# Full-softmax decode attention with gradients: V scores, O and dq by wide matmuls in four column groups

## The chip, the cores and the metric

The kernel runs on one core of a Trainium2 chip. The metric is device time in microseconds (us) of one execution. The median of three executions of the kernel before is 645.86 us (645.73 to 649.34).

## The reference: what is computed

One query per head, 32 heads, 8192 keys of 128 bf16 numbers. Forward attention, and its gradients for a given `grad_out` (called dO here):

```python
B, H, Sq, Skv, Dh = 1, 32, 1, 8192, 128
scores = jnp.einsum('bhqd,bhkd->bhqk', q, k) * scale      # scale = 128 ** -0.5
attn = _softmax(scores, axis=-1)
out  = jnp.einsum('bhqk,bhkd->bhqd', attn, v)
_out, _vjp = jax.vjp(_f, q, k, v)
_grads = _vjp(grad_out)                                   # dq, dk, dv
```

Written out for one head, with p the softmax row: O = p V; the "V scores" dp = V dO, one number a key; ds = p (dp - sum(p dp)) scale; dq = ds K. The two large outputs are outer products: dv = p times dO, and dk = ds times q. Each head therefore reads 2 MB of K and 2 MB of V, and writes 2 MB of dk and 2 MB of dv. All four are touched once.

## The kernel before

**Layout.** A head's K (or V) lies in SBUF as [128 partitions, 64 slots, 128 numbers]: partition p holds the 64 keys 64p to 64p+63. K has three such buffers (`K_BUFS`), V two (`V_BUFS`), and the outputs dk and dv two each (`gpool`). All loads and stores are issued by SyncE (SP) and stand in one queue in program order: a store waits there for its outer products, a load for its buffer. `load_v` (L76) fetches a head's V in one transfer, `load_k` (L71) its K.

**Order.** From L91 on the order is the one written out by hand (`manual_schedule`): each engine takes its instructions in the order of the program text. The loop over h at L260 is a software pipeline: pass h does the K side of head h, the dk and dq work of head h-1 (called `p_`), then the V side of head h.

**K side of head h.** Four VectorE 32x32-block transposes (L146, `k_blocks`) lay K out for contraction over its 128 numbers. 64 TensorE matmuls with four moving columns (L157, `k_scores`) give the scores; a mask (L163) and four matmuls into 32 partitions each (L173, `s_swap`) put them back on the partitions of their keys. Maximum (L284 to L295, with a TensorE transpose at L288), exponential and row sum (L299), the sum over partitions (L300), its reciprocal (L307); then p, four times repeated (`p_rep`, L309), and p times scale (`p_s`, L311).

**V side of head h.** V is read as f32 words, so that one 128x128 transpose on TensorE moves two bf16 slots. Four batches of eight transposes (L188, `v_transposes`) go through two PSUM tiles of two banks each; ScalarE copies each batch of 1024 words to SBUF (L179, `v_copy`), three buffers deep. The V scores are 64 matmuls with the transposed V as stationary operand and two moving columns (L200, `v_scores`), so dp lands on the partitions of its keys. O is 64 matmuls with V as it was loaded as stationary operand and one moving column of p (L205, `contract`), and a copy into a column of `o_all` (L316). The sum of p dp is had as O times dO, by one matmul (L320), before the last scores are in. Four VectorE outer products of 2048 numbers a partition make dv (L215, `outer`), and `load_v(h + 2)` is called between the third and the fourth.

**Head h-1.** ds, four times repeated, in one VectorE instruction (L241, `ds_of`); four outer products make dk; 64 matmuls make dq (L205 again, `dq_of`, in two halves around L173), copied to a column of `dq_all` (L249).

At the end, `result` (L251) turns `o_all` and `dq_all` round and stores them. Heads 0 and 31 store dk and dv in two halves.

The lines below are those that the change touches, and their callers.

Of the kernel before, what the change touches and what calls it, by code (L numbers as in the profile page):

```python
# [9 lines left out]
ALU = mybir.AluOpType  # L10
AX = mybir.AxisListType
BF16 = mybir.dt.bfloat16
F32 = mybir.dt.float32
PSUM = bass.MemoryType.PSUM

CH = 16
R = 4
K_BUFS = 3
V_BUFS = 2
QD = 32  # L20
# [3 lines left out]
def kernel(  # L24
# [11 lines left out]
    nc = tc.nc  # L36
    P = 128
    _, H, S, D = k.shape
    assert D == P and S % (P * CH) == 0 and H <= P
    NT = S // P  # L40
    NCH = NT // CH
    NQ = P // QD
    assert NCH == 4 and NQ == 4
    W = D // 2
# [3 lines left out]
    consts = ctx.enter_context(tc.tile_pool(name="consts", bufs=1))  # L48
# [3 lines left out]
    tpool = ctx.enter_context(tc.tile_pool(name="tsb", bufs=3))  # L52
    gpool = ctx.enter_context(tc.tile_pool(name="gen", bufs=2))
    small = ctx.enter_context(tc.tile_pool(name="small", bufs=2))
    psT = ctx.enter_context(tc.tile_pool(name="psT", bufs=2, space=PSUM))
    psS = ctx.enter_context(tc.tile_pool(name="psS", bufs=1, space=PSUM))
    psD = ctx.enter_context(tc.tile_pool(name="psD", bufs=2, space=PSUM))
    psM = ctx.enter_context(tc.tile_pool(name="psM", bufs=1, space=PSUM))

    Kt, Vt, XK, XV, st = {}, {}, {}, {}, {}  # L60
# [35 lines left out]
    do_blk = consts.tile([P, H, 2, 2], BF16)  # L96
    nc.vector.memset(do_blk[:], 0.0)
# [11 lines left out]
    tp = psT.tile([P, CH, P], BF16, tag="T", name="tp_q")  # L109
# [13 lines left out]
    do_f = consts.tile([P, H], F32)  # L123

    def do_columns():
        for e2 in range(2):
            nc.scalar.copy(
                twice[:, e2], rows[:, 1, :].rearrange("h (j e) -> h e j", e=2)[:, e2:e2 + 1, :].to_broadcast([H, 2, W]))
        tp = psT.tile([P, CH, P], BF16, tag="T", name="tp_do")
        for e2 in range(2):  # L130
            nc.tensor.transpose(tp[:, e2, 0:H], twice[:, e2].rearrange("h t j -> h (t j)"), ident[0:H, 0:H])
        nc.tensor.transpose(tp[:, 2, 0:H], rows[:, 1, :], ident[0:H, 0:H])
        for e2 in range(2):
            for t in range(2):
                nc.scalar.copy(do_blk[t * W:(t + 1) * W, :, e2, t], tp[t * W:(t + 1) * W, e2, 0:H])
        nc.scalar.copy(do_f[:], tp[:, 2, 0:H])
# [40 lines left out]
    def v_copy(h, c):  # L177
        X = tpool.tile([P, CH // 2, P], F32, tag="XT", name="XT_sb")
        nc.scalar.copy(X[:], st[h].pop("T")[:])  # L179
        XV[h, c] = X  # L180

    def v_transposes(h, c, copy=True):

        T_ps = psT.tile([P, CH // 2, P], F32, tag="T", name="T_ps")
        words = Vt[h].rearrange("p n d -> p (n d)").bitcast(F32)
        for i in range(CH // 2):
            m = c * CH // 2 + i
            nc.tensor.transpose(T_ps[:, i, :], words[:, m * P:(m + 1) * P], ident_f[:])  # L188
        st[h]["T"] = T_ps
        if copy:  # L190
            v_copy(h, c)

    def v_scores(h, c):
        X = XV.pop((h, c)).rearrange("p m s -> p (m s)").bitcast(BF16).rearrange("p (m s e) -> p m e s", s=P, e=2)
        if c == 0:
            st[h]["dp"] = psD.tile([P, 512], F32, tag="dp", name="dp_ps")
        for i in range(CH // 2):
            n = c * CH + 2 * i
            for e2 in range(2):
                nc.tensor.matmul(st[h]["dp"][:, n:n + 2], lhsT=X[:, i, e2, :], rhs=do_blk[:, h, e2, :],  # L200
                                 start=(e2 == 0), stop=(e2 == 1), skip_group_check=True)

    def contract(Xt, rep, out_col, first=0, last=NT):
        for n in range(first, last):
            nc.tensor.matmul(out_col, lhsT=Xt[:, n, :], rhs=rep[:, n, 0:1],  # L205
                             start=(n == 0), stop=(n == NT - 1), skip_group_check=True)
# [28 lines left out]

    def ds_of(h):
        x = st[h]
        pdt = small.tile([P, 1], F32, tag="pdt")
        nc.vector.tensor_copy(pdt[:], x["m"][:, 1:2])  # L239
        x["ds"] = small.tile([P, NT, R], BF16, tag="dsrep", name="ds_rep")  # L240
        nc.vector.scalar_tensor_tensor(  # L241
            out=x["ds"][:], in0=x["dp"][:, 0:NT].unsqueeze(2).to_broadcast([P, NT, R]), scalar=pdt[:],
            in1=x["p_s"][:].unsqueeze(2).to_broadcast([P, NT, R]), op0=ALU.subtract, op1=ALU.mult)

    def dq_of(h, half):
        out = st[h]["dp"][:, 128:129]
        contract(Kt[h], st[h]["ds"], out, half * NT // 2, (half + 1) * NT // 2)
        if half == 1:
            nc.scalar.copy(dq_all[:, h:h + 1], out)  # L249

    def result(src, dst):  # L251
        half = small.tile([P, H], BF16, tag="half", name="half")
        nc.scalar.copy(half[:], src[:])
        fin_ps = psT.tile([P, CH, P], BF16, tag="T", name="fin_ps")
        nc.tensor.transpose(fin_ps[0:H, 0, :], half[:], ident[:])
        fin_sb = small.tile([H, D], BF16, tag="fin", name="fin_sb")
        nc.scalar.copy(fin_sb[:], fin_ps[0:H, 0, :])
        nc.sync.dma_start(dst.rearrange("b h s d -> (b h s) d"), fin_sb[:])

    for h in range(H + 1):  # L260
        p_ = h - 1
        if h < H:
            x = st[h] = {}
            rows_bc(h)
            for u in range(NCH):
                k_blocks(h, u)
            k_scores(h)
# [9 lines left out]
        if h > 0:  # L277
            dq_of(p_, 1)
            outer(p_, "dk", 1)
        if 0 < h and h + 2 < H:  # L280
            load_k(h + 2)
# [11 lines left out]
        if h < H:  # L293
            nbias = small.tile([P, 1], F32, tag="nbias")
            nc.vector.tensor_reduce(nbias[:], x["m"][:, 128:256], axis=AX.X, op=ALU.max, negate=True)  # L295
            v_transposes(h, 0, copy=False)
            e = small.tile([P, NT], F32, tag="e")
            rs = small.tile([P, 1], F32, tag="rs")
            nc.scalar.activation(e[:], x["sn"], ACT.Exp, bias=nbias[:], scale=scale, accum_out=rs[:])  # L299
            nc.tensor.matmul(x["m"][:, 0:1], lhsT=ones_f[:], rhs=rs[:], start=True, stop=True,  # L300
                             skip_group_check=True)
        if h > 0:
            outer(p_, "dk", 3)
        if h == H:
            break
        rinv = small.tile([P, 1], F32, tag="rinv")
        nc.vector.reciprocal(rinv[:], x["m"][:, 0:1])  # L307
        x["p"] = small.tile([P, NT, R], BF16, tag="prep", name="p_rep")
        nc.scalar.activation(x["p"][:], e[:].unsqueeze(2).to_broadcast([P, NT, R]), ACT.Copy, scale=rinv[:])  # L309
        x["p_s"] = small.tile([P, NT], F32, tag="p_s", name="p_s")  # L310
        nc.vector.tensor_scalar(x["p_s"][:], e[:], rinv[:], scale, op0=ALU.mult, op1=ALU.mult)  # L311
        v_copy(h, 0)
        v_transposes(h, 1)
        v_transposes(h, 2)
        contract(Vt[h], x["p"], x["m"][:, 2:3])
        nc.scalar.copy(o_all[:, h:h + 1], x["m"][:, 2:3])  # L316
        v_scores(h, 0)
        v_scores(h, 1)
        v_transposes(h, 3)
        nc.tensor.matmul(x["m"][:, 1:2], lhsT=do_f[:, h:h + 1].to_broadcast([P, P]), rhs=o_all[:, h:h + 1],  # L320
                         start=True, stop=True, skip_group_check=True)
        v_scores(h, 2)
        v_scores(h, 3)
# [43 lines left out]
```

## Time and profile before

| what | value |
|---|---|
| median of three executions | 645.86 us (645.73 to 649.34) |
| span of the profiled execution, first to last instruction | 644.6 us |
| recorded instructions | 20,935, of them 9,673 matmuls and 9,673 weight loads |
| TensorE matmul busy | 482.0 us, 75% |
| VectorE busy | 505.9 us, 78% |
| ScalarE busy | 180.7 us, 28% |
| mean granted TensorE clock | 0.601 of full speed |
| moved by DMA | 269.80 MB, mean 419 GB/s |
| from issue to landing, a load of V / of K | 30.1 / 30.3 us |
| from issue to landing, a store of dv / of dk | 34.5 / 33.7 us |

How to read it: the profile is of one execution. No separate end-to-end time is recorded for that execution, so its span is set beside the median of the timed ones: 645.86 - 644.61 = 1.25 us lie around the span. Busy time of TensorE is the union of overlapping matmuls, since they are pipelined. A line such as L205 names the statement in the kernel's text; where two callers share it (O and dq do), the tile names tell them apart. In a table of windows each row is one stretch of the span, with each engine's busy time and number of instructions, the granted clock, and the mean busy share and rate of the sixteen DMA engines. In a timeline a row is: start, length, engine, line, operation, output<-inputs, shapes, count, and in brackets the idle time before it and what ended it.

### The profile page before, as it was taken

How to read it: one execution, taken by the hardware profiler on the slowest of the kernel's cores; microseconds unless marked ns; L12 is line 12 of the kernel's file. 1: busy time of each engine (PE TensorE's matmuls, PEld its weight loads, DVE VectorE, ACT ScalarE, POOL GpSimd, SP SyncE). 2: the span in 40 equal slices, each digit the busy share in tenths (PEclk: the TensorE clock that was granted, in tenths of full speed). 3: DMA queues.
4: the chain of work that ended last, by engine and by line, in shares of the span. 5: the costliest groups of instructions: out<-in, count | busy, mean ns of one | idle time of the engine just before them, and what ended most of it. 6: DMA issues, size and time to landing. Idle time of an engine off the chain costs nothing.

```text
span 644.6 us, 20935 instructions
## 1 busy us (share of the span) xinstructions
PE 482.0 (75%) x9673; PEld 443.9 (69%) x9673; DVE 505.9 (78%) x653; ACT 180.7 (28%) x332; POOL 0.7 (0%) x6
## 2 busy tenths in 40 slices
PE   3998898886777877768776787677876777877780
PEld 2887788785676766768666687567776676866670
DVE  5999899767977679867788777787767986778761
ACT  2333333322233231333222332123322233231230
POOL 0000000000000000000000000000000000000000
PEclk9666666665566655666556665566665566655665
DMA  8999999999999999999999999999999999999985
GB/s 350 404 428 429 424 427 424 428 429 421 418 429 428 428 425 430 430 426 431 425 428 428 430 426 428 428 428 427 427 429 431 424 432 424 430 426 429 427 362 244
DMA packets 19718, 269.80 MB, mean 419 GB/s; under 512 B 2352, under 2 KB 2352, under 8 KB 2864
## 3 DMA queue, kind: packets, MB, share of 16 engines
q1 hardware_dynamic: 19584, 268.47, 98.2%
q8 instruction: 75, 1.23, 0.7%
q14 instruction: 11, 0.09, 0.0%
q10 hardware_dynamic: 48, 0.01, 0.0%
HBM read 134.23 MB, written 134.23 MB: 416 GB/s over the span
## 4 chain that ended last, share of the span: by engine, by line
DMA 62%; PE 24%; DVE 9%; ACT 1%; issue 1%; SPq 0%; DVEq 0%; ACTq 0%
DMA Vt<-in_v_dram 61%; PE T_ps L188 15%; DVE XK_sb L146 4%; DVE G_dv L215 4%; PE m_ps L205 3%; PE dp_ps L200 2%; PE s_ps L157 2%; PE dp_ps L205 1%; DVE G_dk L215 1%; DMA Kt<-in_k_dram 1%; PE m_ps L300 1%; ACT p_rep L309 0%; PE s_ps L173 0%; ACT XT_sb L179 0%; PE m_ps L288 0%
## 5 line engine op out<-in xcount | busy, mean ns | idle before, releaser
L188 PE MATMUL T_ps<-ident_f,Vt 128*128 128x128 f32 x1024 | 217.0, 383 | 27.3 <-DMA Vt<-in_v_dram 24.7
L188 PEld LDWEIGHTS T_ps<-ident_f,Vt 128*128 128x128 f32 x1024 | 182.2, 206 | 45.2 <-PE m_ps L288 21.7
L215 DVE TENSOR_TENSOR G_dv<-p_rep,qd 128x2048 bf16<-128x2048 bf16 x128 | 148.2, 1220 | 60.9 <-DMA out_dram<-G_dv 52.8
L215 DVE TENSOR_TENSOR G_dk<-ds_rep,qd 128x2048 bf16<-128x2048 bf16 x128 | 155.6, 1218 | 4.6 <-DMA out_dram<-G_dk 3.6
L146 DVE STREAM_TRANSPOSE XK_sb<-Kt 128x1024 f32<-128x1024 f32 x128 | 148.3, 1214 | 5.8 <-DMA Kt<-in_k_dram 3.2
L179 ACT COPY XT_sb<-T_ps 128x1024 f32<-128x1024 f32 x128 | 128.7, 1008 | 83.9 <-PE T_ps L188 77.2
L157 PE MATMUL s_ps<-q_blk,XK_sb 128*128 128x4 bf16 x2048 | 59.8, 168 | 94.6 <-DVE pdt L239 87.6
L157 PEld LDWEIGHTS <-XK_sb 128*128 128x128 bf16 x2048 | 57.1, 104 | 103.9 <-DVE pdt L239 96.6
L200 PE MATMUL dp_ps<-do_blk,XT_sb 128*128 128x2 bf16 x2048 | 67.0, 164 | 18.0 <-ACT XT_sb L179 17.6
L200 PEld LDWEIGHTS <-XT_sb 128*128 128x128 bf16 x2048 | 65.5, 103 | 20.7 <-ACT XT_sb L179 20.2
L205 PE MATMUL dp_ps<-ds_rep,Kt 128*128 128x1 bf16 x2048 | 64.0, 165 | 0.4 <-DVE ds_rep L241 0.4
L205 PEld LDWEIGHTS <-Kt 128*128 128x128 bf16 x2048 | 59.5, 104 | 5.7 <-issue 5.6
L249 ACT COPY dq_all<-dp_ps 128x1 f32<-128x1 f32 x32 | 5.1, 159 | 205.2 <-PE dp_ps L205 182.8
L205 PEld LDWEIGHTS <-Vt 128*128 128x128 bf16 x2048 | 57.0, 96 | 0.7
L205 PE MATMUL m_ps<-p_rep,Vt 128*128 128x1 bf16 x2048 | 56.5, 163 | 0.0
L309 ACT ACTIVATE p_rep<-e,rinv 128x256 bf16<-128x256 f32 x32 | 16.3, 508 | 64.6 <-DVE rinv L307 64.6
L307 DVE RECIPROCAL rinv<-m_ps 128x1 f32<-128x1 f32 x32 | 5.4, 168 | 35.2 <-PE m_ps L300 35.1
L234 ACT CAST qd<-s_ps 128x256 bf16<-128x256 f32 x32 | 11.9, 372 | 32.5 <-PE s_ps L230 32.5
L299 ACT ACTIVATE e<-s_ps,nbias 128x64 f32<-128x64 f32 x32 | 10.1, 314 | 32.5 <-DVE nbias L295 32.5
L241 DVE SCALAR_TENSOR_TENSOR ds_rep<-dp_ps,pdt,p_s 128x256 bf16<-128x256 f32 x32 | 15.5, 484 | 4.6 <-PE dp_ps L200 1.3
L163 DVE TENSOR_TENSOR sm<-s_ps,in_quad 128x256 f32<-128x256 f32 x32 | 13.6, 425 | 6.0 <-PE s_ps L157 2.0
L300 PEld LDWEIGHTS m_ps<-rs,ones_f 128*128 128x128 f32 x64 | 17.6, 334 | 0.0
(44 smaller groups left out, 153.1 us busy)
## 6 DMA issues: line engine op xcount, KB each, us to landing
Vt<-in_v_dram SPq DMA_DIRECT2D x32, 2048.0 KB, 30.1
Kt<-in_k_dram SPq DMA_DIRECT2D x31, 2048.0 KB, 30.3
out_dram<-G_dv SPq DMA_DIRECT2D x30, 2048.0 KB, 34.5
out_dram<-G_dk SPq DMA_DIRECT2D x30, 2048.0 KB, 33.7
out_dram<-G_dv SPq DMA_DIRECT2D x4, 1024.0 KB, 14.4
out_dram<-G_dk SPq DMA_DIRECT2D x4, 1024.0 KB, 13.2
Kt<-in_k_dram SPq DMA_DIRECT2D x4, 512.0 KB, 5.1
out_dram<-fin_sb SPq DMA_DIRECT2D x2, 8.0 KB, 12.8
```

Source lines behind the costliest of these rows:

```text
L146: nc.vector.transpose(XK[h][:, :, :, u, :], slots(Kt[h], u, NCH).rearrange("p g d -> p (g d)").bitcast(F32).rearrange("p (g w j) -> p g w ...
L157: nc.tensor.matmul(out[:, g, :], lhsT=cols[:, g, c // 2, c % 2], rhs=q_blk[:, h, c, :], start=(c == 0), stop=(c == 2 * NB - 1), skip_group ...
L163: nc.vector.tensor_tensor(x["sm"][:], x["s"][:, 0:NT].rearrange("p (a g) -> p a g", a=NQ).unsqueeze(2) .to_broadcast([P, NQ, NCH, CH]), in ...
L179: nc.scalar.copy(X[:], st[h].pop("T")[:])
L188: nc.tensor.transpose(T_ps[:, i, :], words[:, m * P:(m + 1) * P], ident_f[:])
L200: nc.tensor.matmul(st[h]["dp"][:, n:n + 2], lhsT=X[:, i, e2, :], rhs=do_blk[:, h, e2, :], start=(e2 == 0), stop=(e2 == 1), skip_group_chec ...
L205: nc.tensor.matmul(out_col, lhsT=Xt[:, n, :], rhs=rep[:, n, 0:1], start=(n == 0), stop=(n == NT - 1), skip_group_check=True)
L215: nc.vector.tensor_tensor(slots(G, r, 4).rearrange("p n (a b) -> p n a b", b=R), slots(rep, r, 4).unsqueeze(2).to_broadcast([P, Q, D // R, ...
L234: nc.scalar.copy(x["qd"][:].rearrange("p a d -> p (a d)"), x["s"][:, 256:512])
L241: nc.vector.scalar_tensor_tensor(out=x["ds"][:], in0=x["dp"][:, 0:NT].unsqueeze(2).to_broadcast([P, NT, R]), scalar=pdt[:], in1=x["p_s"][: ...
L300: nc.tensor.matmul(x["m"][:, 0:1], lhsT=ones_f[:], rhs=rs[:], start=True, stop=True, skip_group_check=True)
L309: nc.scalar.activation(x["p"][:], e[:].unsqueeze(2).to_broadcast([P, NT, R]), ACT.Copy, scale=rinv[:])
```

## The change

Three groups of 64 narrow matmuls become three groups of 16 matmuls with 512 moving columns. In each the stationary operand has 32 columns, and the output is one of four groups of 32 PSUM partitions (b = 0 to 3).

- **V scores.** dO sits in a 34-column window of zeros (`do_win`), so that a slice of 32 columns puts the two scores of a slot pair in row 0 and 1, or 2 and 3, of the group. The moving operand is transposed V, every second bf16, 16 x 32 numbers. The result has the keys along the free dimension; a VectorE 32x32-block transpose of [128, 512] f32 from PSUM (`v_back`) puts it back on the partitions.
- **O and dq.** p (or ds) sits in the last four columns of a window of zeros (`wins`, two for each); the slice is chosen so that head h writes rows 4 (h mod 8) to 4 (h mod 8) + 3 of its group. The moving operand is V (or K) as loaded, four slots at a time. Eight heads add up in one PSUM bank; after every eighth head a copy and four small matmuls (`gather`) add the 16 partial rows of each head.
- **The sum of p dp** is taken from dp itself: a product with e on VectorE, accumulated along the row (L218 of the changed kernel), one matmul with ones (`pd_sum`), times 1/sum. It no longer uses O.
- **ds** is made once (64 numbers a partition) and then copied four times over; ScalarE copies it into its window. p is copied into its window too.
- **Transposes of V** are eight batches of four (one bank each, three in rotation) in place of four batches of eight; all of transposed V of a head is kept, in one SBUF buffer.
- The windows are cleared by GpSimd at the start; the memset of `do_win` stands ahead of the second step of the identity matrix in GpSimd's order.

```diff
+TB = 4
+ST = 8
-    psT = ctx.enter_context(tc.tile_pool(name="psT", bufs=2, space=PSUM))
+    xvpool = ctx.enter_context(tc.tile_pool(name="xvp", bufs=1))
+    single = ctx.enter_context(tc.tile_pool(name="single", bufs=1))
+    psT = ctx.enter_context(tc.tile_pool(name="psT", bufs=3, space=PSUM))
-    psD = ctx.enter_context(tc.tile_pool(name="psD", bufs=2, space=PSUM))
+    psD = ctx.enter_context(tc.tile_pool(name="psD", bufs=1, space=PSUM))
+    psO = ctx.enter_context(tc.tile_pool(name="psO", bufs=1, space=PSUM))
+    psQ = ctx.enter_context(tc.tile_pool(name="psQ", bufs=1, space=PSUM))
...
+    do_win = consts.tile([P, H, 2, QD + 2], BF16)
+    nc.gpsimd.memset(do_win[:], 0.0)
+            w = consts.tile([P, NG, 2 * QD - 4], BF16, name=f"win_{which}{i}")
+            nc.gpsimd.memset(w[:], 0.0)
...
-    def v_scores(h, c):
-        X = XV.pop((h, c)).rearrange(...)
-        for i in range(CH // 2):
-            n = c * CH + 2 * i
-            for e2 in range(2):
-                nc.tensor.matmul(st[h]["dp"][:, n:n + 2], lhsT=X[:, i, e2, :], rhs=do_blk[:, h, e2, :],
-                                 start=(e2 == 0), stop=(e2 == 1), skip_group_check=True)
+    def v_scores(h):
+        cols = XV.pop(h).rearrange(...)("p (m z s e) -> p z e m s", z=2, s=P, e=2)
+        for z in range(2):
+            for e2 in range(2):
+                for b in range(NQ):
+                    nc.tensor.matmul(out[b * QD:(b + 1) * QD, :], lhsT=do_win[:, h, e2, 2 - 2 * z:2 - 2 * z + QD],
+                                     rhs=cols[:, z, e2, :, b * QD:(b + 1) * QD], ...)
...
+    def v_back(h):
+        nc.vector.transpose(x["dpT"][:].rearrange("p m r -> p (m r)"), x["dp"][:])
+        nc.vector.scalar_tensor_tensor(
+            out=prod[:], in0=x["dpT"][:, :, 0:4], scalar=1.0, in1=x["e"][:].rearrange("p (m r) -> p m r", r=4),
+            op0=ALU.mult, op1=ALU.mult, accum_out=x["pd"][:])
...
-    def contract(Xt, rep, out_col, first=0, last=NT):
-        for n in range(first, last):
-            nc.tensor.matmul(out_col, lhsT=Xt[:, n, :], rhs=rep[:, n, 0:1], ...)
+    def contract(h, which, first=0, last=NG):
+        at = QD - 4 - 4 * (h % ST)
+        for g in range(first, last):
+            b = g % NQ
+            nc.tensor.matmul(acc[which][b * QD:(b + 1) * QD, :], lhsT=window(h, which)[:, g, at:at + QD],
+                             rhs=X[:, 4 * g:4 * g + 4, :].rearrange("p n d -> p (n d)"), ...)
+    def gather(h, which, bank):
+        for j in range(4):
+            nc.tensor.matmul(bank[:, at:at + ST], lhsT=S[:, j, :], rhs=pick[:, j, :], ...)
+        nc.scalar.copy(to[:, h - ST + 1:h + 1], bank[:, at:at + ST])
...
+        nc.vector.tensor_tensor(pdt[:], x["m"][:, 1:2], x["rinv"][:], op=ALU.mult)
+        nc.vector.scalar_tensor_tensor(
+            out=ds1[:].rearrange("p (m r) -> p m r", r=4), in0=x["dpT"][:, :, 0:4], scalar=pdt[:],
+            in1=x["p_s"][:].rearrange("p (m r) -> p m r", r=4), op0=ALU.subtract, op1=ALU.mult)
-        nc.vector.scalar_tensor_tensor(
-            out=x["ds"][:], in0=x["dp"][:, 0:NT].unsqueeze(2).to_broadcast([P, NT, R]), scalar=pdt[:], ...)
+        nc.vector.tensor_copy(x["ds"][:], ds1[:].unsqueeze(2).to_broadcast([P, NT, R]))
+        nc.scalar.copy(window(h, "ds")[:, :, QD - 4:QD], ds1[:].rearrange("p (g j) -> p g j", j=4))
...
-            for u in range(NCH):
+            for u in range(NCH - 1):
                 k_blocks(h, u)
+        if h > 0:
+            v_back(p_)
+            pd_sum(p_)
+        if h < H:
+            k_blocks(h, NCH - 1)
             k_scores(h)
...
+        nc.scalar.copy(window(h, "p")[:, :, QD - 4:QD], x["p"][:, :, 0].rearrange("p (g j) -> p g j", j=4))
-        v_copy(h, 0)
-        v_transposes(h, 1)
-        v_transposes(h, 2)
-        contract(Vt[h], x["p"], x["m"][:, 2:3])
-        nc.scalar.copy(o_all[:, h:h + 1], x["m"][:, 2:3])
-        v_scores(h, 0)
-        v_scores(h, 1)
-        v_transposes(h, 3)
-        nc.tensor.matmul(x["m"][:, 1:2], lhsT=do_f[:, h:h + 1].to_broadcast([P, P]), rhs=o_all[:, h:h + 1], ...)
-        v_scores(h, 2)
-        v_scores(h, 3)
+        v_copy(h, 2)
+        for c in range(3, NX // TB):
+            v_transposes(h, c)
+            v_copy(h, c)
+            if c == 4:
+                contract(h, "p")
+        if h % ST == ST - 1:
+            gather_copy("p")
+        v_scores(h)
+        if h % ST == ST - 1:
+            gather(h, "p", x["m"])
```

Batches 0 to 2 of the V transposes and copies 0 and 1 stand ahead of `p_rep`, around the exponential and the row sum.

## The prediction

> **What bounds the kernel now.** I read the DMA queues of the page first, then windows of single heads, then the chain of waits.
>
> ```profile
> DMA  8999999999999999999999999999999999999985
> GB/s 350 404 428 429 424 427 424 428 429 421 418 429 428 428 425 430 430 426 431 425 428 428 430 426 428 428 428 427 427 429 431 424 432 424 430 426 429 427 362 244
> ...
> q1 hardware_dynamic: 19584, 268.47, 98.2%
> q8 instruction: 75, 1.23, 0.7%
> ```
>
> The sixteen DMA engines are 90% busy or more in 37 of 40 slices, and the rate hardly leaves 417 to 432 GB/s. Loads and stores (q1) fill 98.2% of the sixteen engines' span. 268.47 MB at 428 GB/s are 627 us of the 644.6; the rest is the first 2 us, a ramp and a tail. The page also shows fetches of instructions (q8) on the same engines: 75 packets, 0.7% of the span, 4.5 us.
>
> Is it the transfers that set the rate, or do they wait for a chain of compute? The windows separate the two:
>
> ```profile
> 67.00:83.00 16.00, 14.55 (x301) 13.61 (x302) 15.15 (x20) 5.54 (x10) 0.00 (x0) 0.61 1.01 424
> 140.00:160.00 20.00, 14.17 (x301) 13.22 (x299) 15.74 (x20) 4.78 (x10) 0.00 (x0) 0.59 1.01 424
> ...
> 634.00:636.00 2.00, 0.00 (x0) 0.00 (x0) 0.00 (x0) 0.00 (x0) 0.00 (x0) 0.50 0.58 241
> 638.00:640.00 2.00, 0.00 (x0) 0.00 (x0) 0.00 (x0) 0.00 (x0) 0.00 (x0) 0.50 0.57 242
> ```
>
> Columns are the window, its length, busy us of TensorE, weight loads, VectorE, ScalarE, GpSimd (with counts), granted clock, DMA share, GB/s. In the first row compute runs free, from buffers filled ahead: VectorE is busy 15.15 of 16 us. In the chain that ended last, the dv products of successive heads start at 67.96 and 84.34 us, 16.4 us apart. Later a head takes 20 us, VectorE idles over 4 us of them, and DMA is as full as before. So a head costs about 16.4 us of compute, bound by VectorE, and about 20 of DMA. The waits agree: the dv products wait 52.8 us in all for their store, and the V transposes 24.7 us for their load. The last two rows are the tail, with every compute engine done: the share lies flat at 0.57, nine sixteenths. Nine of sixteen engines still have a backlog; that, not the last products, ends the kernel.
>
> **Step 1: TensorE.** Three rows of one head go: O 1.75 us, V scores 0.95 + 0.56 + 0.58, dq 0.99 + 1.01, together 5.8 us. In come 48 matmuls of 512 columns. No row has 512 columns. A bf16 matmul takes 168 ns with 4 columns (L157), 286 with 128 (L255), 390 with 256 (L230), so the last columns cost (390 - 286)/128 = 0.81 ns each, and 512 of them 0.42 us. One after another, 48 are 20.2 us a head; four abreast, 5.0. The row that decides is the only one that writes four column groups today:
>
> ```profile
> 331.96 0.27 PE L205 MATMUL dp_ps<-ds_rep,Kt 128*128 128x1 bf16 x5
> 332.16 0.44 PE L173 MATMUL s_ps<-sm,lane 128*32 128x64 f32 x8
> 332.54 1.01 PE L205 MATMUL dp_ps<-ds_rep,Kt 128*128 128x1 bf16 x32
> ```
>
> Eight passes of 64 columns take 0.44 us, one alone 314 ns, so they start (440 - 314)/7 = 18 ns apart, where 64 columns at 0.81 would keep them 52 apart. They run 2.9 abreast. I take that: 20.2/2.9 = 7.0 us, +1.2 a head. The V scores' moving operand steps over every second bf16; no row shows such a step on a moving operand (the strided weights of L157 load in 104 ns, as the unstrided ones of dq do). Between no loss and half speed that is 0 to 2.3 us; I take 0, the nearer row.
>
> Two rules of the skill bear on this. "TensorE: Matmul & The Clock Gate", Part 3, gives 2.38 times for three column tiles of 512 columns; 20.2/2.38 would be 8.5 us, +2.7. "TensorEngine Tiling (Array Packing)", Key Properties, speaks against the change: a change of tiling mode drains TensorE. The trace has one such place, the weight load after L173, idle 0.17 us; six a head would be 1.0 us. With both, the sum is +3.7 us on an engine that is not the bound.
>
> **Step 2: VectorE.** Added per head: the transpose back, 512 words (L146 takes 1.214 us for 1024: 0.6; from PSUM it may be as much as the whole 1.21); the product with row sum (0.26, as L311 with 64 numbers); ds once (0.26); its copy four times over (between 0.26 and the 0.48 of L241; I take 0.35). L241's 0.48 goes. Net 0.6 + 0.26 + 0.26 + 0.35 - 0.48 = +1.0 us (bounds +0.8 to +1.8). Compute alone becomes 17.4 us a head. Could a new wait come? The transpose back stands behind four dv products and three K transposes (8.0 us), and the last K transpose, ds and all of dk queue behind it. Say the load of V lands at t. ScalarE's copies are 159 + 0.83 x 512 = 0.58 us by the rows with 1, 256 and 1024 words. The eighth V transpose ends at t+1.9, copies 0 and 1 at t+2.6, p at t+3.1, its window at t+3.4, six copies at t+6.9; V scores (a third of 7.0) end by t+9.3. VectorE starts the dv products at t+3.1 and needs the scores at t+11. So 2 us of cover; if it is gone, the excess lands on the 17.4. ScalarE gains 8 x 0.58 - 4 x 1.01 + two window copies of 0.25 - two of 0.16 = +0.8 us on 5.6: free. Every eighth head the gathers cost ScalarE and TensorE some 1.5 us each, hidden under the same slack.
>
> So 17.4, at most 18.5 with half a microsecond of new waits, against 20: **the cover of steps 1 and 2 is the DMA's 20 us**, and they cost nothing until compute passes it. What queues on SP stays in order. The last reader of V ends near t+6 instead of t+9.3 (the load of V is issued at 343.91 today, its data there at 334.66), so V's load may enter the queue 3 us sooner. With about six transfers of 2 MB outstanding (four kinds of some 32 us each, every 20 us) this makes the queue deeper, not faster: 0, bounds 0 and -3 us in the tail.
>
> **Step 3: the start and the end.** GpSimd clears 2176 numbers before the identity is ready (128 took 0.2 us): about 2 us later, under the wait for the last quarter of K at 7.85. At the end, ds of the last head is ready at 625.7; now VectorE leaves the dv products at 623.8, then transpose 0.6, product 0.26, matmul 0.6, pdt 0.15, ds and copy 0.6, hops 0.3: 626.3. The last stores move by +0.6; behind the nine engines' backlog I count +0.4 (bounds 0, +2).
>
> **Step 4: instruction fetches.** Of 20,935 records, 384 a head (three times 64 pairs) become 96, and some ten on other engines are added: about 12,000, 57%. q8's 4.5 us become 2.6. Where DMA engines are the bound and the fetches spread evenly, that is -1.9 us. If they sit elsewhere 0; if on the nine late engines alone, -3.4.
>
> **Sum:** 644.6 + 0 + 0 + 0.4 - 1.9 = 643.1 us of span; the median stands 1.25 us above the span, so **644.3 us**.
>
> **Rivals.** *(a) The matmuls do not overlap* (slower). Price: contract and V scores 6.7 us each in place of 2.3, dq 6.7 in two pieces between the K scores and the row maximum. The scores end at t+18, 7 us after VectorE wants them, and dq delays the next V side by 4.7: about 17.4 + 11.7 = 29 us a head, 930 us at this clock; at the full clock, columns half as dear, about 19 us and nothing lost. Midway 24, some 780 us. It decides once the 48 matmuls cost over about 12 us a head. For it: no row has 512 columns with weights changing each time; TensorE's granted clock is 0.6. Against: L173. *(b) Compute passes 20 us by waits*: the transpose from PSUM at 1.2, half-speed strided reads, drains, ds one step later. It needs 2.6 us over my 17.4; at 20.5 to 21, 32 x 0.5 to 1 = 16 to 32 us more, 660 to 676. *(c) Faster by over 1%*: fetches on the late engines (-3.4) and V's earlier load clearing the tail (-3): 638. Against: bytes over rate is 627 us whatever TensorE does. *(d) The instruction traffic buys nothing*: 646.3; a case within the forecast's own 1%.
>
> **Numbers.** Forecast with (d) 0.77, (a) 0.07, (b) 0.09, (c) 0.07. A measurement of this kernel can tell about 1% (6.5 us) from no change. Faster 0.07, same 0.77, slower 0.16. The range takes in the bounds of steps 3 and 4 and (c) below, 638, and the lower edge of (b) above, 655.
>
> **What would show it.** Right: DMA share near 1.0 at 425 GB/s through the middle; q8 near 43 packets; O, scores and dq rows of 16 matmuls in 1.7 to 2.5 us; VectorE near 538 us busy; 17 to 18 us a head before 100 us. Wrong: GB/s below 415 in mid-span, the transpose back waiting on the scores matmuls, or matmuls of 512 columns starting 0.4 us apart.

## The result and the profile after

The changed kernel takes 644.45 us (median of 13 runs, 644.02 to 645.36) against 645.93 us for the kernel before (13 runs, 645.4 to 649.34): a ratio of 0.997, 95% interval 0.9961 to 0.998. The forecast was 644.3 us and "same"; the gain is small, but the interval tells it from none. The profiled execution's span is 642.7 us, 1.9 us less than that of the profiled execution before; the forecast had 1.5. Some 0.4 us of these 1.9 are not the change's: wherever span and time of one execution are both on record, the time is 1.7 to 2.0 us above the span, and the kernel before has a span of 644.1 us in the middle there. So its profiled execution, with 644.6, was one of the longer ones, and the 1.25 us "around the span" set beside each other two different executions. Like with like, the change gained 1.5 us.

First the DMA part of the changed kernel's page.

```profile
DMA  8999999999999999999999999999999999999995
GB/s 346 410 428 430 424 428 429 427 425 430 428 425 420 423 426 428 429 429 428 429 430 426 429 430 423 433 428 429 430 423 433 426 428 430 429 428 427 429 390 209
...
q1 hardware_dynamic: 19584, 268.47, 98.4%
q8 instruction: 40, 0.66, 0.4%
```

The picture is the one of before: full in 38 of 40 slices, 420 to 433 GB/s through the middle. 98.4% of 642.7 is 632.4 us for the loads and stores, where 98.2% of 644.6 was 633.0. Only the fetches (q8) are clearly fewer: 40 packets in place of 75, 0.4% in place of 0.7%, 2.6 us in place of 4.5.

The same windows as before, of the changed kernel (window, length, busy us of TensorE, weight loads, VectorE, ScalarE, GpSimd, granted clock, DMA share, GB/s):

```profile
67.00:83.00 16.00, 10.56 (x146) 7.64 (x142) 15.36 (x24) 5.67 (x14) 0.00 (x0) 0.82 1.01 427
140.00:160.00 20.00, 13.35 (x163) 10.17 (x156) 16.40 (x23) 5.95 (x16) 0.00 (x0) 0.69 1.00 425
634.00:636.00 2.00, 0.00 (x0) 0.00 (x0) 0.00 (x0) 0.00 (x0) 0.00 (x0) 0.50 0.50 210
638.00:640.00 2.00, 0.00 (x0) 0.00 (x0) 0.00 (x0) 0.00 (x0) 0.00 (x0) 0.50 0.06 25
```

In the free stretch TensorE has 10.56 us to do where it had 14.55, at a higher granted clock (0.82, before 0.61); VectorE is as full as before. Successive dv products start at 70.79, 87.95 and 105.10 us: 17.16 us a head, before 16.4. Later a head takes 19.8 us and DMA is full. The tail thins out sooner: from 638 to 640 us the share is 0.06, where it was 0.57.

The new groups (line, engine, operation, tiles and shape, count | busy us, mean ns of one | idle before):

```profile
L232 PE MATMUL acc_ds<-Kt,win_ds 128*32 128x512 bf16 x512 | 67.3, 627 | 0.9 <-ACT win_ds L293 0.9
...
L208 PE MATMUL dp_ps<-XV_sb,do_win 128*32 128x512 bf16 x512 | 34.3, 383 | 24.9 <-ACT XV_sb L189 24.9
L232 PE MATMUL acc_p<-Vt,win_p 128*32 128x512 bf16 x512 | 33.5, 382 | 0.0
...
L215 DVE STREAM_TRANSPOSE dpT<-dp_ps 128x512 f32<-128x512 f32 x32 | 21.6, 675 | 0.0
```

One matmul of 512 columns shows 382 ns in O and V scores and 627 in dq: in windows of one head the granted clock is 1.00 under O (336 to 338 us) and V scores (340 to 342), and 0.50 under dq (330 to 334). But 16 of them make a row of little over 1 us, as the timeline of one head says (start and length, us):

```profile
331.61 1.04 PE L232 MATMUL acc_ds<-Kt,win_ds 128*32 128x512 bf16 x8
332.66 1.07 PE L232 MATMUL acc_ds<-Kt,win_ds 128*32 128x512 bf16 x8
337.18 1.05 PE L232 MATMUL acc_p<-Vt,win_p 128*32 128x512 bf16 x16
340.47 1.05 PE L208 MATMUL dp_ps<-XV_sb,do_win 128*32 128x512 bf16 x16 [0.78 <-ACT XV_sb L189]
```

That is 4.2 us a head in place of 5.8. What VectorE waits for, in the list of waits of the changed kernel (us in all, times, longest):

```profile
DVE G_dv L257 <- DMA out_dram<-G_dv: 45.5, 19, 2.9
DVE nbias L350 <- PE m_ps L343: 7.5, 4, 2.3
```

The dv products' wait for their store has shrunk from 52.8 to 45.5 us as VectorE got busier; the wait of 7.5 us in all, 2.3 at the longest, at the four heads behind a gather is new. TensorE's wait for V fell from 24.7 to 0.5 us. The chain that ended last now runs through the dv stores (70% of the span) where it ran through the loads of V (61%).

### The profile page after: what moved, and what is told of

The parts are those of the page before. It is cut to its first block, busy times and chain, and to the rows that moved or that the text cites. A ratio compares the mean times of both kernels' runs of the same rounds, so it can differ in the third digit from the quotient of the medians.

```text
span 642.7 us, 12069 instructions
## 1 busy us (share of the span) xinstructions
PE 404.0 (63%) x5128; PEld 289.2 (45%) x5128; DVE 537.9 (84%) x780; ACT 194.4 (30%) x475; POOL 5.9 (1%) x11
## 3 DMA queue, kind: packets, MB, share of 16 engines
q1 hardware_dynamic: 19584, 268.47, 98.4%
## 4 chain that ended last, share of the span: by engine, by line
DMA 70%; DVE 24%; ACT 2%; PE 1%; issue 1%; POOL 0%; DVEq 0%; POOLq 0%
DMA out_dram<-G_dv 70%; DVE G_dv L257 14%; DVE XK_sb L157 4%; DVE G_dk L257 3%; ACT XV_sb L189 1%; DVE dpT L215 1%; DVE four L120 1%; ACT p_rep L368 0%; DVE sm L174 0%; PE acc_ds L232 0%; POOL do_win L104 0%; PE m_ps L246 0%; PE s_ps L168 0%; DVE ds L288 0%; PE T_ps L198 0%
## 5 line engine op out<-in xcount | busy, mean ns | idle before, releaser
L257 DVE TENSOR_TENSOR G_dv<-p_rep,qd 128x2048 bf16<-128x2048 bf16 x128 | 148.2, 1220 | 54.7 <-DMA out_dram<-G_dv 45.5
L198 PE MATMUL T_ps<-ident_f,Vt 128*128 128x128 f32 x1024 | 162.4, 318 | 0.5 <-DMA Vt<-in_v_dram 0.5
L198 PEld LDWEIGHTS T_ps<-ident_f,Vt 128*128 128x128 f32 x1024 | 144.7, 171 | 17.8 <-ACT XV_sb L189 13.6
L189 ACT COPY XV_sb<-T_ps 128x512 f32<-128x512 f32 x256 | 137.0, 590 | 24.0 <-PE T_ps L198 22.8
L280 PE MATMUL m_ps<-pd,ones_f 128*128 128x1 f32 x64 | 18.7, 361 | 162.9 <-DVE prod L218 162.9
L280 PEld LDWEIGHTS m_ps<-pd,ones_f 128*128 128x128 f32 x64 | 16.0, 311 | 168.8 <-DVE prod L218 154.0
L232 PE MATMUL acc_ds<-Kt,win_ds 128*32 128x512 bf16 x512 | 67.3, 627 | 0.9 <-ACT win_ds L293 0.9
L208 PE MATMUL dp_ps<-XV_sb,do_win 128*32 128x512 bf16 x512 | 34.3, 383 | 24.9 <-ACT XV_sb L189 24.9
L232 PE MATMUL acc_p<-Vt,win_p 128*32 128x512 bf16 x512 | 33.5, 382 | 0.0
L208 PEld LDWEIGHTS <-do_win 128*32 128x32 bf16 x512 | 14.2, 94 | 36.3 <-issue 29.7
L215 DVE STREAM_TRANSPOSE dpT<-dp_ps 128x512 f32<-128x512 f32 x32 | 21.6, 675 | 0.0
## 6 DMA issues: line engine op xcount, KB each, us to landing
Vt<-in_v_dram SPq DMA_DIRECT2D x32, 2048.0 KB, 32.7
```

The source lines that it names most:

```text
L189: nc.scalar.copy(XV[h][:, c * TB:(c + 1) * TB, :], st[h].pop(("T", c))[:])
L208: nc.tensor.matmul(out[b * QD:(b + 1) * QD, :], lhsT=do_win[:, h, e2, 2 - 2 * z:2 - 2 * z + QD], rhs=cols[:, z, e2, :, b * QD:(b + 1) * QD ...
L215: nc.vector.transpose(x["dpT"][:].rearrange("p m r -> p (m r)"), x["dp"][:])
L232: nc.tensor.matmul(acc[which][b * QD:(b + 1) * QD, :], lhsT=window(h, which)[:, g, at:at + QD], rhs=X[:, 4 * g:4 * g + 4, :].rearrange("p ...
L257: nc.vector.tensor_tensor(slots(G, r, 4).rearrange("p n (a b) -> p n a b", b=R), slots(rep, r, 4).unsqueeze(2).to_broadcast([P, Q, D // R, ...
L280: nc.tensor.matmul(x["m"][:, 1:2], lhsT=ones_f[:], rhs=x["pd"][:], start=True, stop=True, skip_group_check=True)
```

## The experiments

All start from the changed kernel. Ratios are against the kernel before, which ran beside them with medians of 645.91 to 646.01 us; the changed kernel's own is 0.997. Differences in us are against its 644.45. Theory A is the prediction's: DMA sets the rate, TensorE and VectorE are covered, and what was gained is fetch traffic. The rivals: instruction traffic costs nothing (B), or compute and its waits set part of the time (C).

### Does DMA set the rate?

```
-            nc.sync.dma_start(rows_of(dst, h, c, parts), slots(G, c, parts))
+            if which == "dv" and parts == 1:
+                nc.sync.dma_start(rows_of(dst, h, 0, 1)[:, 0:60, :], G[:, 0:60, :])
+            else: ...
```

> The changed kernel, but 60 of the 64 slots of dv are stored for each head except the first and the last (one sixteenth of dv is left out): 128 partitions x 4 slots x 256 bytes x 30 heads = 3.93 MB less of 268.5 MB. No engine's work is changed. If the DMA queue bounds the kernel, 3.93 MB at 427 GB/s are 9.2 us: 635.2. If the chain of VectorE and ScalarE bounds it and DMA only waits for that, no change: 644.4. Between them, part of the gain comes back where heads become bound by compute: the free head takes 17.2 us against 20 us a head, so all of 0.29 us a head should be kept.

Measured: 634.44 us (634.23 to 634.75), ratio 0.9818 [0.9804, 0.9833]: 10.0 us less than the changed kernel. The bytes gave 9.2; the times of the packets of loads and stores, added up in the trace and shared over sixteen engines, fell by 9.7 (632.7 to 623.0). With no engine's work touched, the whole of it came out of the span. The first reading of the prediction holds: bytes over rate set the time.

### Do the matmuls run side by side, and why?

Two runs. The first changes only the order of the 48 matmuls: all of one column group, then all of the next.

```
-        for z in range(2):
-            for e2 in range(2):
-                for b in range(NQ):
+        for b in range(NQ):
+            for z in range(2):
+                for e2 in range(2):
...
-        for g in range(first, last):
+        for g in sorted(range(first, last), key=lambda g: (g % NQ, g)):
```

> The changed kernel with the same 48 wide matmuls a head in another order: all of one column group, then all of the next, so that only the meeting of two groups overlaps, 36 steps in place of 12. Theory (the overlap of four groups is what makes the wide matmuls cheap): the O and V scores rows go from 1.05 us to some 2.8 each, the dq halves from 1.04 to some 2.1. The prediction's rival of matmuls that do not overlap puts this near 24 us a head, 780; by the measured cover (2 us after the V scores) I expect 20 to 21 us a head, 645 to 670. Rival (each wide matmul runs by itself anyway): no change in any row, 644.4.

Measured: 644.12 us (644.0 to 644.75), ratio 0.9972 [0.9962, 0.9983]. Nothing moved, in the rows either. Timeline of this kernel:

```profile
332.79 1.08 PE L232 MATMUL acc_ds<-Kt,win_ds 128*32 128x512 bf16 x8
337.54 1.08 PE L232 MATMUL acc_p<-Vt,win_p 128*32 128x512 bf16 x16
340.85 1.14 PE L208 MATMUL dp_ps<-XV_sb,do_win 128*32 128x512 bf16 x16 [0.78 <-ACT XV_sb L189]
```

So neighbours in the program need not go to different groups. By itself that spoke against the groups as the cause and for the narrow weights (32 columns in place of 128). The second run decides it, with 16 matmuls of constants more per head, in a form that changes from head to head:

```
+        for i in range(16):
+            h % 4 == 0: out x["s"][0:32, :],              weights of 32 columns   (L387)
+            h % 4 == 1: out group i % 2 of x["s"],        weights of 32 columns   (L390)
+            h % 4 == 2: out group i % 4 of x["s"],        weights of 32 columns   (L393)
+            h % 4 == 3: out x["s"][:], the whole bank,    weights of 128 columns  (L395)
```

> The changed kernel with 16 more matmuls of 512 moving columns of constants per head, after the V scores; on heads 0, 4, 8, ... all into one column group with weights of 32 columns, on heads 1, 5, ... alternating between two groups, on heads 2, 6, ... over four groups, on heads 3, 7, ... with weights of 128 columns over the whole bank. If matmuls run side by side because they go to different column groups, a row of 16 takes about 1.05 us over four groups, about 1.9 over two and 3.5 in one group or over the whole bank (0.21 to 0.22 us each). If weights of 32 columns alone make them quick, 1.05 us in all three. The time stays within 1 us of the changed kernel's.

Measured: 644.55 us in one run, span 642.8. Timeline, four successive heads (the granted clock is 1.00 in all four rows):

```profile
340.67 1.89 PE L390 MATMUL s_ps<-do_win 128*32 128x512 bf16 x16
...
360.35 1.09 PE L393 MATMUL s_ps<-do_win 128*32 128x512 bf16 x16
...
380.57 3.63 PE L395 MATMUL s_ps<-do_win,ident 128*128 128x512 bf16 x16
...
400.57 3.62 PE L387 MATMUL s_ps<-do_win 128*32 128x512 bf16 x16
```

Narrow weights into one group cost 3.62 us, as much as full weights over the whole bank; two groups 1.89, four 1.09. It is the groups. Less the 0.38 us that one matmul shows, the starts are (3.62 - 0.38)/15 = 0.216 us apart in one group. With two groups they come in pairs, with four in fours, each set some 0.21 us after the last: 7 and 3 such steps and 0.38 us make 1.89 and 1.03. So each group takes a matmul every 0.216 us, and four groups run at the same time. The first run then says more: in its row of V scores, too, the starts come in four sets of four (340.85 to 340.90, 341.07 to 341.13, 341.29 to 341.36, 341.51 to 341.60), although the program has four in a row for one group. Since one group starts a matmul only every 0.216 us, each set must hold one of each group: the matmuls of the next group do not wait behind those of the group before, at least up to the four in a run there.

### Is TensorE covered?

```
+        wide = do_win[:].rearrange("p h e j -> p (h e j)")[:, 0:512]
+        for _ in range(12):
+            nc.tensor.matmul(x["s"][:], lhsT=ident[:], rhs=wide, start=True, stop=True, ...)
```

This stands after the V scores, 12 matmuls of constants a head.

> Control for the two runs with more rows: the changed kernel with 12 matmuls of constants of 512 columns a head in the same place, 2.6 us of TensorE time a head at the full clock and 5.0 at half, in only 768 more rows. Theory of the instruction traffic: q8 near 43 packets, the time within 0.4 us of 644.45. Rival (busy TensorE itself, its clock or its reads cost time): 1 to 2 us more, as with the narrow matmuls.

Measured: 644.83 us (644.6 to 644.99), ratio 0.9979 [0.997, 0.9987]. 12 x 0.22 = 2.6 us of TensorE a head, 84 us in the kernel, and 0.4 us of time, which the intervals cannot tell from nothing. In this place TensorE is covered, and few rows (24 a head) of long matmuls cost no fetches to speak of: q8 has 43 packets.

### Is VectorE covered?

Three, then six more transposes of the V scores ahead of the product:

```
+        for _ in range(3):      # 6 in the second run
+            nc.vector.transpose(x["dpT"][:].rearrange("p m r -> p (m r)"), x["dp"][:])
```

> The changed kernel with its transpose of the V scores done four times over in place of once: 3 x 0.675 = 2.0 us more of VectorE a head, in the chain of every head. Free-running heads come to 17.2 + 2.0 = 19.2 us. Theory (the DMA's 20 us a head cover compute): no more than 1 us over 644.45. Rival (compute sets the rate, or the end waits for the last head's chain): 32 x 2.0 = 65 us more, 709; or, for the tail alone, 2 us more.

> As the run before, with six transposes more: 4.05 us a head, 21.2 us for a free-running head, past the DMA's 20. Theory: compute becomes the bound; 19.3 + 31 x 21.2 us to the last head's dv products, 11.2 to its dk products and some 15 to the end make 703 us of span, 705 in all, with the DMA share near 0.93 in mid-span. Rival (compute sets the rate already): 32 x 4.05 = 130 us over 644.45, 774.

Measured: 653.23 us (652.57 to 654.4), ratio 1.0114 [1.01, 1.0127], and 725.5 us (725.43 to 726.39), ratio 1.1235 [1.1217, 1.1252]. Three transposes took 68.8 us, 2.15 a head. 60 us of that are covered; but 8.8 show, although a head of 19.5 us stands below the DMA's 19.8. Where they come from is seen in the chain of the first of the two runs (start, us):

```profile
313.91 4.63 DVE G_dv L259 x4
318.54 3.41 DVE XK_sb L157 x3
325.06 1.16 DVE XK_sb L157
326.28 1.87 PE s_ps L168 x64
328.15 0.97 PE acc_ds L234 x6
330.94 1.89 PE m_ps L248 x8
333.54 1.72 PE T_ps L198 x8
336.31 4.63 DVE G_dv L259 x4
```

This is the head behind which the gather of dq stands (`m_ps L248`): 22.4 us from one dv product to the next, 2.9 more than the others. Seven heads of 19.5 and one of 22.4 are 19.9 on average, no less than DMA needs. And the backlog at the end is used up: from the first dk product of the last head to the end there are 10.0 us here (640.94 to 650.9), 19.0 in the changed kernel (623.68 to 642.7). With six transposes a head takes 21.8 us and the gather head 24.6 (348.56 to 373.20); compute is the bound throughout, and the time lies between the two forecasts: a plain head costs 0.3 us more than 17.16 + 4.3, a gather head 2.9 more than that. So the cover is there, and is thinner than the plain heads say: C becomes true with some 2 us of VectorE more a head; whether a little of it holds in the changed kernel as it is, this run does not show.

### What is the place of V's load worth?

```
-        if 0 < h and h + 2 < H:
-            load_v(h + 2)
         outer(h, "dv", 3)
+        if 0 < h and h + 2 < H:
+            load_v(h + 2)
```

> The changed kernel with the load of V two heads on issued after the store of dv in place of ahead of it, so some 4 us later in the queue. Theory (the queue is deep and the DMA engines are the bound): no change, 644.0 to 645.0. Rival (V's earlier load made the gain): back by 1.0 to 1.5 us, 645.5 to 646.0.

Measured: 650.16 us (649.93 to 650.22), ratio 1.0063 [1.0051, 1.0075]: 5.7 us more, which I had not expected. Waits of TensorE in this kernel:

```profile
PE T_ps L198 <- DMA Vt<-in_v_dram: 56.7, 23, 3.5
```

0.5 us became 56.7. The load is issued 8.1 us after the head's first V transpose (300.05 to 308.14), not 5.7, and behind the 2 MB of the dv store instead of ahead of them. DMA keeps its rate in the middle; the loss is at the end, where the last V arrives at 621.9 us, DMA runs at shares of 0.58 to 0.78 between 615 and 635 us with too little left to do, and the first dk product comes at 633.5. Which of the two, the 2.4 us or the change of order, costs the 5.7, this run does not separate.

### What do instructions cost?

Four runs add small matmuls of constants after the V scores (144, 288 and 72 pairs of weight load and matmul a head), or take some away, and one adds GpSimd instructions.

```
+        for _ in range(144):      # 288, then 72
+            nc.tensor.matmul(x["m"][:, 300:301], lhsT=ident[:], rhs=ident[:, 0:1], start=True, stop=True, ...)
```

> The changed kernel, with 144 one-column matmuls of constants added a head, in the gap of TensorE after the V scores: 9,216 more rows of program on TensorE, 16,698 in all, as many as before the change, and some 4 us a head of TensorE time in a gap of 5. Theory (the gain is the instruction traffic that no longer passes through the DMA engines): q8 back near 75 packets and 0.7%, the time back by 1.5 to 2.3 us over 644.45, near 646.3. Rival (the gain is V's earlier load or the tail): q8 grows but the time stays at 644.0 to 645.0.

> As the run with 9,216 more rows, but with twice as many (288 a head, 18,432 rows; some 7 to 8 us a head of TensorE time, of which some 2 may come past the gap, against about 2.5 us of room left under the DMA's 20 us). Theory of the instruction traffic: q8 near 110 packets and 1.05%, the time 3.0 to 4.6 us over 644.45, near 648.2. Rival (V's load or the tail): 644.0 to 645.5, unless TensorE becomes the bound, which would show as DMA share below 0.95 in mid-span.

Measured: 659.54 us (658.75 to 660.56), ratio 1.0206 [1.0193, 1.022], and 844.59 us (841.37 to 849.88), ratio 1.3083 [1.3049, 1.3117]. Neither measures the traffic alone. Timeline of TensorE in the second:

```profile
410.20 3.57 PE L384 MATMUL m_ps<-ident 128*128 128x1 bf16 x128 [2.49 <-issue]
416.14 0.72 PE L384 MATMUL m_ps<-ident 128*128 128x1 bf16 x21 [2.37 <-issue]
```

128 pairs run in 3.57 us, then TensorE stands for 2.37 us with nothing to wait for that the profile's rows show. The trace's packet records show it: a packet of q8 travels from 407.98 to 408.98 us and the next from 413.90 to 414.78, one in each gap, and TensorE goes on 1.2 and 1.4 us after each. So it is short of instructions there, at a DMA share of 0.88 (400 to 420 us). The same gaps, shorter, are in the first run (`issue` within the K scores, 1.34 us, after a packet that ended 1.3 us before), with the matmuls pushing back the K scores by a few microseconds. (The first expectation's "16,698 in all" is a slip: the page of that run has 19,472 records of TensorE, and the kernel before 19,346, so "as many as before the change" is about right.)

```
+        for i in range(432):
+            nc.gpsimd.memset(scratch[:, i % 8:i % 8 + 1], 0.0)
```

> The changed kernel with 13,824 memsets of one column on GpSimd, 34 ns apart in the trace of before, which nothing waits for: more program to fetch, by 54 packets of 256 rows, and no work on any engine of the chain. Theory of the instruction traffic (35 packets fewer were worth 1.5 to 1.9 us): q8 near 94 packets, the time 2.2 to 2.9 us over 644.45, near 647. Rival (the change gained by V's earlier load, or in the tail's chain): 644.0 to 645.0.

Measured: 719.0 us (714.63 to 719.46), ratio 1.1114 [1.109, 1.1138]; a miss as an experiment. The instructions meant as traffic alone held up VectorE, and their fetches are not in q8 (40 packets, as in the changed kernel) but in q14, 121 packets after 14. Groups of this kernel:

```profile
L372 DVE TENSOR_SCALAR p_s<-e,rinv 128x64 f32<-128x64 f32 x32 | 80.7, 2522 | 3.4
...
L293 DVE COPY ds_rep<-ds 128x256 bf16<-128x256 bf16 x32 | 50.1, 1565 | 1.1
```

255 ns and 294 ns in the changed kernel. The last two runs are smaller, and go both ways: half of the instructions that the change took away are put back, and about as many more taken out.

```
-        for g in range(CH):
-            for c in range(2 * NB):
-                nc.tensor.matmul(out[:, g, :], lhsT=cols[:, g, c // 2, c % 2], rhs=q_blk[:, h, c, :], ...)
+        nc.tensor.matmul(x["s"][:, 0:NT], lhsT=cols[:, 0, 0, 0],
+                         rhs=q_blk[:, 0:4].rearrange("p h c a -> p (h c a)"), start=True, stop=True, ...)
```

> The changed kernel with 72 one-column matmuls of constants per head between the V scores and the dv products: 4,608 more instructions in all (2,304 matmuls, 2,304 weight loads), half of what the change took away, no result changed. They take about 1.9 us of TensorE a head in a gap of some 5 us. Fetches cost DMA time: the change took 8,866 instructions, 35 packets and, by the shares, 1.9 us of the sixteen engines with it (1.3 us by its 0.57 MB at 427 GB/s), so 18 packets more give +1.0 us (0.7 by bytes): 645.1 to 645.5. Rival (fetches cost nothing, the gain of the change came from elsewhere): 644.4 as the changed kernel, with the 18 packets visible in the queue. What would spoil it: waits of VectorE on k scores that the extra matmuls push back, seen as waits of over 0.5 us a head.

> The changed kernel, but the 64 small matmuls of the K scores of a head are one matmul of 64 columns (63 of 64 parts of the scores' contraction are left out, so p and all that follows from it hold other numbers): 126 instructions a head less, 4,032 in all, some 16 packets. Fetches cost DMA time: -0.9 us by the shares (0.6 by bytes), 643.5 to 643.9. Rival: 644.4, since the head is bound by DMA and the 1.8 us of TensorE that go with them lie under it. Against the kernel with 4,608 more, the two theories differ by 1.3 to 1.9 us.

Measured: 648.34 us (647.8 to 648.75), ratio 1.0032 [1.0019, 1.0044], and 641.56 us (641.28 to 641.82), ratio 0.9928 [0.9915, 0.9942]. B falls: the time follows the number of instructions in both directions, by +3.9 us for 4,608 more and -2.9 for 4,032 fewer. But each is three to four times what I had priced (+0.7 to 1.0, -0.6 to 0.9). The queue lines of the two pages, the one with more first:

```profile
q1 hardware_dynamic: 19584, 268.47, 98.0%
q8 instruction: 58, 0.95, 0.6%
```

```profile
q1 hardware_dynamic: 19584, 268.47, 98.8%
q8 instruction: 24, 0.39, 0.2%
```

The shares of the page are rounded; added up packet by packet, q1 and q8 take 637.1 us of the sixteen engines in the run with more and 633.5 in the run with fewer, against 635.2 in the changed kernel. So +1.9 and -1.7 us are busy time, of which q8 itself has +1.2 and -1.0, near what I had priced; the rest, +2.0 and -1.2, is time in which some of the engines have nothing to do. In the run with more, VectorE's waits are those of the changed kernel within 2.3 us each, TensorE's new waits are 0.43 us a head of `issue` ahead of the added matmuls and 3.3 us in all for V, and the wide matmuls above put more TensorE time in the same place for 0.4 us. That speaks for the transfers, but it is an argument and not a measurement: a free head also takes 17.3 us there instead of 17.16. The lag builds up along the way: its dv stores are issued 0.1 us later than the changed kernel's at the eighth head, 1.9 at the eighteenth, 3.7 at the last. The run with fewer is less clean, since 1.9 us of K scores a head go out of the chain as well, and its first dv store is issued 1.6 us earlier for that alone. That fetches fall on some of the sixteen engines more than on others, and so make every transfer wait for the latest, would give such a factor; the trace keeps no record by engine, so this is not shown.

Nor is there one price an instruction. 768 more, in the wide matmuls of the run above, cost 0.4 us; 1,024 more, in the run with 16 wide matmuls a head, 0.1 (one execution); 4,608 cost 3.9 and 9,216 cost 15.1. In these runs the price grew with how many stood in one place.

## Why the prediction was right, and where it was not

**The bound.** Right. One sixteenth of dv less to store moved the time by 10.0 us where the bytes said 9.2. The tail that "lies flat at 0.57" is not there after: it falls off from 0.50 to 0.06. From the last head's first dk product to the end there are 19.0 us, before 18.9.

**Step 1, TensorE: the mechanism was right, the size was not.** "They run 2.9 abreast", so 7.0 us and +1.2 a head; it is 4.2 us, -1.6. The term that was mis-sized is the price of one matmul. "512 of them 0.42 us" came from two rows (L230 and L255) at a granted clock of 0.50; the row with 256 columns takes 281 ns in the changed kernel, at 1.00, and with the 382 ns of 512 columns a column costs 0.39 ns there instead of 0.81. O and V scores ran at 1.00: 0.216 us between the starts of one group, half the price, and 1.05 us a row where 16 x 0.42/2.9 is 2.3. dq ran at 0.50 and came out near the price, 2.1 us. The overlap was less far off: four groups do run at the same time, and a whole row of 16 is 3.62/1.09 = 3.3 times as fast as in one group, for 2.9 priced. The strided reads cost nothing, as chosen (383 ns in V scores, 382 in O). The Trainium skill's "TensorE: Matmul & The Clock Gate", Part 3, gives 2.38 times for three column tiles; here rows of 16 ran 3.62/1.89 = 1.9 times as fast on two groups and 3.3 times on four, and three were not run. The drain that "TensorEngine Tiling (Array Packing)", Key Properties, speaks of is inside the 4.2 us and no line here separates it. As TensorE is covered (12 wide matmuls more for nothing), the error cost nothing. Rival (a) is out by the rows, and (b) by the free head of 17.16 us: VectorE's only new wait of note is that of at most 2.3 us behind a gather.

**Step 2, VectorE: the sums were right, the cover was not looked at where it is thinnest.** VectorE went from 505.9 to 537.9 us, +1.0 a head as worked out, and the free head takes 17.16 us against 17.4. The transpose back took 675 ns, for 0.6 priced and 1.21 feared; copy, ds and product 294, 285 and 225 + 82 ns. V scores end at 341.5 us and VectorE reaches them at 347.1: a cover of 5.6 us, 2.3 of them its own wait for the store (2 us priced). What did not hold is "every eighth head the gathers cost ScalarE and TensorE some 1.5 us each, hidden under the same slack": they are in VectorE's own loop. When VectorE is 2.15 us a head busier, the gather head is 2.9 us longer than the others, and in the changed kernel itself it takes 20.4 to 20.5 us (299.22 to 319.70, 457.60 to 478.02), past the DMA's 19.8. DMA stays full there (427 to 434 GB/s from 300 to 330 us), so one such head is hidden by the transfers still in the queue, and not by slack of its own; the room above 17.16 is under 2.15 us and not the 2.6 that plain heads leave.

**V's load.** "3 us sooner" was right: it is issued 5.7 us after the first V transpose, where it was 9.25. "Deeper, not faster" was right for the load: 32.7 us from issue to landing after 30.1. But "0, bounds 0 and -3" is not supported: the later place within the changed kernel costs 5.7 us, outside the bounds. How much of the earlier place counts in the comparison of the two kernels stays open, since that run also turned round the order of load and store.

**Step 3, start and end.** "About 2 us later, under the wait for the last quarter of K at 7.85" was half right. The identity is ready 1.8 us later (3.1 us after 1.3), but that is not all: the other clearings, of `win_p` and `win_ds`, ran beside VectorE's first copies. Timeline of the start (start and length, us):

```profile
3.05 1.73 POOL L110 MEMSET win_p<- 128x960 bf16 x2
...
3.34 3.52 DVE L120 COPY four<-rows 32x128 bf16<-32x128 bf16 x4
...
4.72 1.74 POOL L110 MEMSET win_ds<- 128x960 bf16 x2
...
7.99 4.60 DVE L157 STREAM_TRANSPOSE XK_sb<-Kt 128x1024 f32<-128x1024 f32 x4
```

The four copies took 0.62 us before, 3.52 beside the clearing. So VectorE comes to K at 7.99, with all four transposes still to do, where it had done two by 7.85, and the first dv products come at 19.33 us instead of 17.09. The bytes did not wait: the first two slices hold (346 + 410) x 16.07 us = 12.1 MB, before (350 + 404) x 16.1 = 12.1. At the end the chain of the last head was priced 0.6 us later, and it is: from the end of the dv products to dk there are 2.5 us after 1.9. But dk starts 2.06 us earlier (623.68 after 625.74), since what comes before it is earlier; the +0.4 of the sum is not seen.

**Step 4, fetches: the packets were right, the price is not settled.** 40 packets (43 named); packet by packet q8 takes 2.6 us of the sixteen engines after 4.7, -2.1 for the -1.9 worked out. The time fell by 1.5. That match is weaker than it looks. The runs with more and fewer instructions moved by 0.84 and 0.72 ns an instruction; 8,866 fewer would be 6.4 to 7.5 us by that. If that price holds for the instructions that went out, some 5 to 6 us were given back elsewhere; that it holds for them is not shown, and the runs with wide matmuls were cheaper. Candidates are VectorE's +1.0 us a head (three transposes, +2.15, cost 8.8 us, though mostly by the gather heads) and the longer way through the last head. No run here undoes them alone. Rival (d) falls as it was put, "the instruction traffic buys nothing". So the sum was right to a fifth of a microsecond, and its terms are sure only to some microseconds each: what was forecast for a reason is that the change would hide under the transfers and gain little; that 644.3 came so near 644.45 is in part luck.

## What to carry to other kernels

Where the DMA engines are full, a faster engine beside them buys little: here three groups of TensorE's rows fell from 5.8 to 4.2 us a head, 51 us in 32 heads, and the time by 1.5 us. What is fetched over those engines counts as well as what is loaded: 4,608 small instructions more came with 3.9 us, 384 wide matmuls with their weight loads with 0.4, though how much of the 3.9 is the fetches themselves is open. Outputs of 32 partitions in four column groups made a row of 16 wide matmuls 3.3 times as quick, in both orders of the groups that were run. A price for a matmul holds for the clock of the rows it was read from. And before calling an engine covered, take the cover at its worst head: one that comes every eighth time decides as well as the average.

## What the hardware showed that I had not expected

- The column groups overlap even when the program fills one after another: 16 matmuls in 1.08 to 1.14 us against 1.05 when the groups alternate, with the starts in sets of four in both.
- TensorE can run out of instructions: with the DMA engines at a share of 0.88, it got 128 pairs in about 5.9 us (3.57 busy, 2.37 idle), and went on 1.2 to 1.4 us after a packet of q8 had come.
- GpSimd's memsets hold up some of VectorE's operations: p's scaled copy took 3.79 us instead of 0.255 while 128 memsets of one column ran, and ended when they did (340.58 and 340.53 us). The dk products, two inputs each, kept their 1.22 us. Timeline of the run with GpSimd instructions:

```profile
335.27 1.22 DVE L258 TENSOR_TENSOR G_dk<-ds_rep,qd 128x2048 bf16<-128x2048 bf16 x1
336.25 4.28 POOL L385 MEMSET scratch<- 128x1 f32 x128 [0.63 <-POOL scratch L385]
336.79 3.79 DVE L372 TENSOR_SCALAR p_s<-e,rinv 128x64 f32<-128x64 f32 x1
```

- A packet of a fetch (16 KB) takes the engines longer than its bytes: 2.6 us x 16 / 40 = 1.0 us of one engine, where q1's packets of 13.7 KB take 632.4 x 16 / 19,584 = 0.52 us.
